# Attention's side work cut into pieces of three matmuls, spread over all 128 steps of an octet, and the last octet run block by block through both of its groups

## The chip, the cores and the metric

The kernel runs on one core of one Trainium2 chip. The metric is the device time of one execution in microseconds; the time before is 2678.99 us, the median of 3 runs (2677.80 to 2679.76). Engines are named as in the profile: PE is TensorE (PEld its weight loads), ACT is ScalarE, DVE is VectorE, POOL is GpSimd, and SP is the engine whose queue issues nearly all DMAs.

## The reference

Four residual layers on x of 2048 tokens by 512 features (32 heads of 16): softmax attention (A), hedgehog linear attention (B), A, B. Each layer is x + layer(layernorm(x)).

```python
# A
qkv = (x @ wqkv).reshape(B, S, 3, H, Dh).transpose(2, 0, 3, 1, 4)
p = softmax(einsum("bhqd,bhkd->bhqk", q, k) * Dh ** -0.5)
o = einsum("bhqk,bhkd->bhqd", p, v).transpose(0, 2, 1, 3).reshape(B, S, D) @ wo
# B
phi(t) = concat[softmax(t @ w_phi), softmax(-(t @ w_phi))]        # per head
kv = einsum("bhsf,bhsd->bhfd", phi(k), v);  z = sum over s of phi(k)
o = (phi(q) @ kv) / (phi(q) @ z + 1e-6) @ wo
```

The change touches layer A alone, which runs twice.

## The kernel before, in words

**Steps.** Layer A works on four *octets* of 8 heads. An octet has two *groups* of 4 heads, g = 2o (even heads) and g = 2o+1 (odd heads). A group goes through 4 blocks of 512 queries (`j`), and each block through 16 tiles of 128 keys (`kt`). One (g, j, kt) is a *step*; an octet has 128 steps, a layer 512. In a step, `scores` issues four matmuls `s<-kq` in two halves (two heads each, in the two row halves of the array), and ACT takes one exponential of 128x1024 for each half (`p<-s`). The halves go round three PSUM buffers (`psS`, `bufs=3`), the exponentials' results round six SBUF buffers. `pvs` then issues the four matmuls `pv<-p,v` of the step two back (`LAG = 2`); the trace records each as two. The 16 steps of a block add up in one PSUM bank, `pv`. After the last of them `norm` turns it around on DVE (`yt`, `rec`, `yn`), and for an odd group writes the octet's part of the attention's output (`yb`, `osp`) to DRAM, or for the last octet into `ob`. The bank is single: the next block's first `pv` matmul waits until DVE has read it (`yt`).

**Side work.** PE's order inside the attention is written out by hand (`tc.manual_schedule(engines={E.PE})`), while DVE, POOL and SP are ordered by a scheduler. Between the steps PE does other work in pieces. It comes from generators in the queue `self.fill`; `pump(1)` runs the first one up to its next `yield`. There are three kinds:

- `octet(o+1)`, during octet o: the values of the next octet's 8 heads (4 blocks of 48 matmuls of 128x128, `pv_`), then its keys and queries (8 projections of 12 matmuls of 128x512, `pqk`). A projection is read by DVE (`tq`, then the high half and the low half in `stg`), POOL squares the high half (`sq`), and one small matmul sums the squares per head (`psn`), which DVE reads (`km` or `sh`). `pqk`, `psn`, `pv_`, `po` and `pst` share one PSUM bank (tag "M").
- `tail(j, ob)`, in the last octet: the output projection of block j (4 tiles of 12 matmuls of 128x512, `po`), the residual (`xt`), the next layer's norm on DVE, and four transposes per tile (`pst`).
- `extra`, in the first layer alone: layer B's weights are folded and split (`prep_ao`, `prep_b`): 8 times four transposes (`bps`) and four fp32 matmuls (`bpf`) on PE, and a long run of work on DVE.

**Where the pieces stand before.** `values` yields after every 8 matmuls and once after its evacuation: 7 pumps a block, 28 in all. `project` yields after every 2, then there are three pumps without projection work, the third of which does `psn`: 9 a projection, 72 in all. An octet has thus 100 pumps, one in each of its steps 0 to 99; steps 100 to 127 have none. The tails yield every 4 matmuls. The last octet runs all of group 6 (steps 0 to 63) and then group 7 (64 to 127); a tail needs both groups of its block, so the first one starts at step 82, and block 3's is done after the attention, inside layer B's start (`nxt.feed`). `extra` starts in step 114 of the octet before.

**Loads of keys and queries.** `alloc_pairs` takes two SBUF tiles for a group's keys and queries (`kq`), `load_rows` copies rows of `stg` into them (12 DMAs) and `load_shift` four rows of `sh`. For the next octet's even group both were emitted in step 112, for its odd group at the start of that octet.

Of the kernel before, what the change touches and what calls it, by code (L numbers as in the profile page):

```python
# [33 lines left out]
LAG = 2  # L34
E = mybir.EngineType
COMPUTE = {E.PE, E.DVE, E.Activation, E.Pool}
# (part of the stationary side, part of the moving side): 0 = high, 1 = low half
# [4 lines left out]
def mha_hedgehog_stack(ctx, tc, x_in, a_wqkv, a_wo, b_wqkv, b_wphi, b_wo, out, shmin=SHMIN):  # L42
# [29 lines left out]
    # ones on the 16 rows of each head of an octet, column per head  # L72
# [7 lines left out]
    def peak_of(v, u, engine=None):  # L80
        """Bound on |v| per partition: the maximum, on the scalar engine the sum; v [P, 2048], its half u or all."""
        if u is not None:
            v = v[:, u * 1024:(u + 1) * 1024]
        m = sp.tile([P, 1], F32, name="pk")
        if engine is nc.scalar:
            junk = pp.tile([P, 1024], F32, tag="p", name="pkj")
            nc.scalar.activation(junk, v, AF.Abs, accum_out=m)
        else:
            nc.vector.tensor_reduce(m, v, AX.X, ALU.max, apply_absolute_value=True)
# [22 lines left out]
    def split(dst, src, sc):  # L112
        """dst[0] + dst[1] = src * sc, both fp16."""
# [30 lines left out]
    # rows 48..63 of each head's half: SHROW on the key side, 0 on the query side  # L144
# [14 lines left out]
    def prep_a():  # L159
        """The first layer up to its attention; splits wqkv on the side."""  # L160
# [12 lines left out]
        def octet(o):  # L173
            """High parts, and the scaled weights for the low parts."""
# [112 lines left out]
    # head order of B's columns: (octet, parity, four)  # L287
# [56 lines left out]
    class Norm:  # L344
# [8 lines left out]
        def stats_parts(self, t0, n, soon=False):  # L353
            """Mean and 1/deviation of tiles t0 .. t0+n-1."""
# [51 lines left out]
        def turned(self, t, n, ps):  # L406
            """Tiles t .. t+n-1, ps [P, n, 512]."""
# [27 lines left out]
        def half(self, t2):  # L435
            """As soon as two more tiles are there."""
# [58 lines left out]
    def norm2(ps, dst):  # L495
        """Both parities of an octet at once, ps [P, 2, 512]."""
# [13 lines left out]
    def o_block(j, ob, wo, co, x_src, x_dst, box, after=None, wide=True, early=False):  # L510
        """box receives the 4 new token tiles, after is called for each two.
        early: the first two tiles begin with the octets that come first."""
        for t2 in range(2):
# [12 lines left out]
            for u in range(0 if early and t2 == 0 else 2):  # L526
                t = 2 * t2 + u
                n = 0
                for a, b in PASSES:
                    yield  # L530
                    if n == 0:
                        ps = ps2[:, u, :] if wide else psum1("po")
                    for c in range(NC4):
                        nc.tensor.matmul(ps, ob[:, c, a, t * P:(t + 1) * P], wo[:, b, c, :], start=(n == 0), stop=(n == 11))  # L534
                        n += 1
# [14 lines left out]
    def v_block(xnT, wv, j):  # L550
        """Values of 4 token tiles, [V_h | 1] per head."""
# [19 lines left out]
    okt = cp.tile([32, 8], F32, name="okt")  # L571

    class LayerA:
# [14 lines left out]
        def start_octet(self, o, w):  # L588
            # [V_h | 1] per token tile and head
# [7 lines left out]
                stg=stgp.tile([P, 4, S], F16, tag="stg", name="stg"),  # kl, kh, qh, ql  # L597
# [4 lines left out]
        def project(self, o, j, ps, ten):  # L602
            n = 0
            for a, b in PASSES:
                for c in range(NC4):
                    nc.tensor.matmul(ps, self.oct[o]["w"][:, a, ten, c, :], self.xnT[j][:, b, c, :], start=(n == 0), stop=(n == 11))  # L606
                    n += 1
                    if n % 2 == 0:
                        yield

        def values(self, o, j, ps):
            """Values of 512 tokens for the octet's heads."""
            q = self.oct[o]
            n = 0
            for t in range(4):
                for a, b in PASSES:
                    for c in range(NC4):
# [3 lines left out]
                        if n % 8 == 0:  # L621
                            yield
# [43 lines left out]
        def octet(self, o):  # L666
            """Queries and keys of 8 heads, one PSUM bank at a time."""
            self.start_octet(o, self.next_w or self.octet_w(o))
            self.next_w = None
# [5 lines left out]
            for j in range(NJ):  # L675
                for ten in (1, 0):
                    ps = psum1("pqk")
                    yield from self.project(o, j, ps, ten)
# [8 lines left out]
                    yield  # L687
# [32 lines left out]
        def feed(self, lns, work):  # L720
            """All that comes before the attention; work[j]: pieces of other work around block j."""
# [106 lines left out]
        def tail(self, j, ob):  # L828
            xts = []
            ln = Norm(xts, f"a{self.li}_{j}")  # L830
            yield from o_block(j, ob, self.wo, con["oA"], self.x_src, self.x_dst, xts, ln.half, wide=False)
# [12 lines left out]
        def attention(self, extra, nxt):  # L844
            """All heads; returns the next layer's normalised input blocks as they are emitted."""
            state["att"] = True
            self.fill, self.pt, self.out = deque(), {}, []
            pend = deque()
            with tc.manual_schedule(engines={E.PE}):
                for g in range(8):  # L850
                    for k in range(NJ * NT):
                        j, kt = k // NT, k % NT
                        self.scores(g, j, kt)
                        pend.append((g, j, kt))
                        if len(pend) > LAG:
                            self.pvs(*pend.popleft())
                        if g % 2 == 0 and g < 6:
                            if k == 0:
                                if g:
                                    self.alloc_pairs(g + 1)  # L860
                                    self.load_pairs(g + 1)
                                self.fill.append(self.octet(g // 2 + 1))
                            self.pump(1)
                        elif g < 6:
                            if k < 48:
                                self.pump(1)
                            if k == 48:
                                while self.fill:
                                    self.pump(1)
                                self.alloc_pairs(g + 1)  # L870
                                self.load_pairs(g + 1)
                        if g == 5 and k == 50 and extra is not None:
                            self.fill.append(extra())
                        if g == 6:
                            if k == 8:
                                self.alloc_pairs(7)
                                self.load_pairs(7)
                            if k == 48:
                                self.wo = load_hl(dAo, "woA")
                                nxt.begin()  # L880
                        if g > 5 or (g == 5 and k > 50):
                            self.pump(1)
# [15 lines left out]
    class LayerB:  # L898
# [15 lines left out]
        def feed(self, j, xnT, between=lambda t: None):  # L914
            """Features and values of 512 tokens, summed into the state."""
# [66 lines left out]
        def expo(self, ps):  # L982
            """exp(x - max) and exp(min - x) per head."""
# [11 lines left out]
        def part_sums(self, f, r, factor):  # L995
            """factor / sum for the softmaxes r of a tile."""
# [7 lines left out]
        def share(self, f, factor):  # L1004
            """Both softmaxes of each head, times factor."""
# [3 lines left out]
        def halves(self, f):  # L1009
            """f = fk[0] + fk[1] in fp16."""  # L1010
# [6 lines left out]
        def share_split(self, f, low):  # L1017
            """share and halves for the last keys, in two parts side by side; low goes between."""
# [250 lines left out]
```

## Time and profile before

| | |
|---|---|
| median of 3 runs | 2678.99 us |
| span of the profiled execution | 2678.6 us |
| PE busy | 2555.4 us (95%) |
| ACT busy | 2214.8 us (83%) |
| DVE busy | 995.5 us (37%) |
| first layer A, its attention | 85.3 to 1101.7 us |
| second layer A, its attention | 1415.6 to 2419.4 us |

A matmul's end is modelled in this trace, and matmuls overlap: the useful number for PE is the distance from one start to the next, not the duration. A row of the timeline gives the start, the time it covers, engine, line, operation, output and inputs, shape and count. A row of the windows gives the stretch, its length, then busy time and count per engine, the granted share of the TensorE clock, the DMA share and GB/s. Time that an engine spends idle is named with what ended it, in brackets behind a row.

### The profile page before, as it was taken

To read this page: it belongs to the slowest core of one execution; us is meant where nothing else is said; L and a number is where in the kernel's file an instruction comes from. 1 tells how busy PE (TensorE), PEld (TensorE's weight loads), DVE (VectorE), ACT (ScalarE), POOL (GpSimd) and SP (SyncE) were. 2 spreads that over 40 slices of the span, in tenths; PEclk is the share of its full clock that TensorE was granted. 3 is DMA by queue.
4 is the path that set the end of the run, shared out by engine and by line. 5 is a ranking of instruction groups with operands and counts; after the bars stand their busy time and mean duration, and the time that the engine had idled before them with its cause. 6 is when DMAs were issued, how large, how long until landed. Compare 5 with 4: busy or idle time off the path is not lost.

```text
span 2678.6 us, 44388 instructions
## 1 busy us (share of the span) xinstructions
PE 2555.4 (95%) x18080; PEld 761.5 (28%) x18080; DVE 995.5 (37%) x1896; ACT 2214.8 (83%) x2442; POOL 373.6 (14%) x502
## 2 busy tenths in 40 slices
PE   6999999999999999999889999999999999999998
PEld 4321131122113122355343112211221111224543
DVE  6212112311224315689861122112112200248997
ACT  5799999999998997554438999999999999874552
POOL 3000000000000000266430000000000000004552
PEclk9999999999999999999999999999999999999999
DMA  4500310130122403100143004002200320121003
GB/s 150 102 29 13 51 30 9 17 56 9 48 32 73 127 27 99 40 24 9 65 103 67 4 14 64 9 9 40 41 5 29 62 50 1 36 72 48 9 17 104
DMA packets 48551, 120.05 MB, mean 45 GB/s; under 512 B 9872, under 2 KB 10768, under 8 KB 45136
## 3 DMA queue, kind: packets, MB, share of 16 engines
q1 hardware_dynamic: 47664, 114.75, 18.4%
q8 instruction: 144, 2.36, 0.4%
q0 software_dynamic: 672, 2.36, 0.2%
q14 instruction: 71, 0.58, 0.1%
HBM read 60.06 MB, written 31.59 MB: 34 GB/s over the span
## 4 chain that ended last, share of the span: by engine, by line
PE 61%; ACT 16%; DVE 14%; issue 6%; POOL 2%; DMA 0%; ACTq 0%; POOLq 0%; DVEq 0%
PE pv L811 26%; PE s L796 16%; ACT p L799 15%; PE pqk L606 6%; PE po L534 5%; DVE su L998 2%; PE pbv L927 1%; PE pk L927 1%; POOL f L1007 1%; DVE f L990 1%; DVE f L991 1%; DVE st L359 1%; DVE mx L987 1%; PE pq L927 1%; DVE su L999 1%
## 5 line engine op out<-in xcount | busy, mean ns | idle before, releaser
L799 ACT ACTIVATE p<-s 128x1024 f32<-128x1024 f32 x2048 | 1922.4, 1197 | 101.3 <-PE s L796 61.3
L811 PE MATMUL pv<-p,v 128*32 128x512 f32 x8192 | 1091.3, 605 | 2.9 <-DVE yt L473 2.8
L796 PE MATMUL s<-kq 64*128 64x512 f16 x4096 | 686.7, 383 | 39.6 <-DMA kq<-sh 3.3
L796 PEld LDWEIGHTS <-kq 64*128 64x128 f16 x4096 | 153.8, 94 | 720.7 <-issue 701.3
L473 DVE STREAM_TRANSPOSE yt<-pv 128x512 f32<-128x512 f32 x64 | 45.9, 716 | 768.8 <-PE pv L811 768.5
L811 PEld LDWEIGHTS pv<-p,v 128*32 128x32 f32 x8192 | 161.6, 108 | 360.6 <-issue 334.0
L633 POOL TENSOR_TENSOR sq<-stg 128x512 bf16<-128x512 f16 x48 | 71.1, 1481 | 1133.9 <-DVE stg L683 1052.0
L1007 POOL TENSOR_TENSOR f<-f,su 128x1024 f32<-128x1024 f32 x62 | 119.9, 1934 | 594.5 <-DVE su L1001 566.5
L682 DVE TENSOR_SCALAR tq<-pqk,c_qk 128x512 f32<-128x512 f32 x48 | 35.5, 740 | 324.1 <-PE pqk L606 324.1
L927 PEld LDWEIGHTS <-xnTa 128*128 128x128 f16 x1152 | 110.4, 98 | 137.8 <-DVE f L991 15.8
L606 PEld LDWEIGHTS <-wA 128*128 128x128 f16 x768 | 52.2, 99 | 277.0 <-issue 257.8
L606 PE MATMUL pqk<-xnTb,wA 128*128 128x512 f16 x384 | 110.2, 388 | 1.1 <-ACT xnTb L426 1.1
L606 PE MATMUL pqk<-xnT,wA 128*128 128x512 f16 x360 | 104.2, 383 | 3.9 <-DVE xnT L429 2.0
L927 PE MATMUL pbv<-wbv,xnTa 128*128 128x512 f16 x384 | 88.6, 379 | 12.1 <-DVE f L991 12.1
L534 PE MATMUL po<-woA,ob 128*128 128x512 f16 x384 | 97.0, 381 | 0.7 <-DVE ob L490 0.7
L992 ACT ACTIVATE f<-f,c_pB 128x1024 f32<-128x1024 f32 x64 | 72.6, 1148 | 29.7 <-DVE f L991 29.6
L1013 ACT ACTIVATE fk<-f 128x1024 f16<-128x1024 f32 x30 | 31.7, 1057 | 74.8 <-POOL f L1007 74.8
L927 PE MATMUL pk<-wbqk,xnTa 128*128 128x512 f16 x384 | 88.4, 379 | 0.0
L927 PE MATMUL pq<-wbqk,xnTa 128*128 128x512 f16 x384 | 88.4, 379 | 0.0
L998 DVE TENSOR_REDUCE su<-f 128x64 f32<-128x1024 f32 x64 | 77.5, 1211 | 9.5 <-ACT f L992 8.8
L1039 ACT ACTIVATE qT<-pqt 128x512 f32<-128x512 f32 x64 | 34.6, 592 | 54.1 <-PE pqt L1038 54.1
L534 PE MATMUL po<-wbo,obB 128*128 128x512 f16 x336 | 75.6, 385 | 3.3 <-DVE xnTb L429 3.3
(261 smaller groups left out, 1892.4 us busy)
## 6 DMA issues: line engine op xcount, KB each, us to landing
kq<-stg SPq DMA_DIRECT2D x168, 128.0 KB, 5.0
xd<-xt SPq DMA_DIRECT2D x24, 512.0 KB, 3.0
xt<-xd SPq DMA_DIRECT2D x24, 512.0 KB, 3.6
kq<-dC SPq DMA_DIRECT2D x64, 128.0 KB, 3.6
oD<-osp SPq DMA_DIRECT2D x24, 256.0 KB, 2.0
ob<-oD SPq DMA_DIRECT2D x8, 768.0 KB, 5.4
xt<-in_A_x_dram SPq DMA_DIRECT2D x8, 512.0 KB, 3.7
wbqk<-dBqk SPq DMA_DIRECT2D x2, 2048.0 KB, 8.9
```

What stands on the lines that cost most here:

```text
L473: nc.vector.transpose(yt.rearrange("p a b -> p (a b)"), ps)
L534: nc.tensor.matmul(ps, ob[:, c, a, t * P:(t + 1) * P], wo[:, b, c, :], start=(n == 0), stop=(n == 11))
L606: nc.tensor.matmul(ps, self.oct[o]["w"][:, a, ten, c, :], self.xnT[j][:, b, c, :], start=(n == 0), stop=(n == 11))
L633: nc.gpsimd.tensor_tensor(sq, hi, hi, ALU.mult)
L682: nc.vector.tensor_scalar(tq, ps, cqk, CLAMP, op0=ALU.mult, op1=ALU.min)
L796: nc.tensor.matmul(s[:, u, :], t[r:r + 64, 0, kt * P:(kt + 1) * P], t[r:r + 64, 1, j * 512:(j + 1) * 512], start=True, stop=True)
L799: nc.scalar.activation(pt, s, AF.Exp, scale=0.25 / (QS * QS))
L811: nc.tensor.matmul(acc[32 * hh:32 * hh + 32, :], self.oct[o]["v"][:, r:r + 32], pt[:, hh % 2, :], start=(kt == 0), stop=(kt == NT - 1), sk ...
L927: nc.tensor.matmul(dst, xnT[:, a, c, t * P:(t + 1) * P], w(b, c), start=(i == 0 and c == 0), stop=(i == 2 and c == NC4 - 1))
L992: nc.scalar.activation(f, f, AF.Exp, scale=con["pB"])
L998: nc.vector.tensor_reduce(su, f[:, r, :], AX.X, ALU.add)
L1007: nc.gpsimd.tensor_tensor(f3, f3, self.part_sums(f3, slice(0, 64), factor), ALU.mult)
```

## The change

1. `project` takes a `piece`; in the attention it is 3 instead of 2, and the last piece no longer ends in a pump of its own, so the evacuation by DVE follows the last matmul in the same pump. One of the two empty pumps between the evacuation and `psn` goes. A projection has 5 pumps instead of 9.
2. `values` yields after every 12 matmuls instead of 8: 4 pumps a block instead of 7. An octet has 56 pumps.
3. A counter, `credit`, grows by 56/116 each step, and a pump runs when it reaches 1: one in about 2.07 steps, up to step 118 (`FILLED`), where what is left is done at once.
4. In the last octet the order of the steps is block by block: block 0 of group 6, block 0 of group 7, block 1 of group 6 and so on. The first tail starts at about step 34. The tails of blocks 0 to 2 use pieces of 3 matmuls, block 3's of 4 as before; a pump comes in 0.65 of the steps.
5. Each octet's weights are loaded one octet ahead (`next_w`). The first 1536 columns of the next even group's rows are loaded once blocks 0 to 2 are projected, the rest and the shifts are emitted at step 118. Group 7 is loaded there too, and `extra` starts there.

The diff's core (comments and docstrings went as well, which moves the line numbers by 2 to 7):

```diff
-        def project(self, o, j, ps, ten):
+        def project(self, o, j, ps, ten, piece=2):
...
-                    if n % 2 == 0:
+                    if n % piece == 0 and n < 12:
                         yield
...
-                        if n % 8 == 0:
+                        if n % 12 == 0 and n < 48:
                             yield
...
-            self.start_octet(o, self.next_w or self.octet_w(o))
-            self.next_w = None
+            self.start_octet(o, self.next_w)
+            self.next_w = self.octet_w(o + 1) if o < 3 else None
...
                     sq = self.square(hi)
                     yield
-                    yield
                     self.norms(o, j, sq, ten)
+                    if j == 2 and ten == 0:
+                        self.alloc_pairs(2 * o)
+                        self.load_rows(2 * o, slice(0, 1536))
                     yield
...
+            credit = 0.0
+            order = [(g, j, kt) for g in range(6) for j in range(NJ) for kt in range(NT)]
+            order += [(g, j, kt) for j in range(NJ) for g in (6, 7) for kt in range(NT)]
...
+                    if o < 3:
+                        if k == 0:
+                            if o:
                                 self.alloc_pairs(g + 1)
                                 self.load_pairs(g + 1)
+                            self.fill.append(self.octet(o + 1))
+                        if k == FILLED:
+                            while self.fill:
+                                self.pump(1)
+                            self.load_rows(2 * o + 2, slice(1536, S))
+                            self.load_shift(2 * o + 2, slice(0, S))
...
+                        credit += 56 / (FILLED - 2)
+                    else:
...
+                        credit += 0.65
+                    if credit >= 1:
+                        credit -= 1
+                        self.pump(1)
```

What stands on PE in octet 1 of the first layer, where a projection's piece lies between two steps; `kq3` is the odd group's tile. Before, one step has the piece between its `pv` and the next step's scores:

```order
L811 MATMUL pv_4566<-p_4541,v1_1008 32x512 x2
L606 LDWEIGHTS wA_3299
L606 MATMUL pqk_4530<-xnT0_2_139,wA_3299 128x512
L606 LDWEIGHTS wA_3299
L606 MATMUL pqk_4530<-xnT0_2_139,wA_3299 128x512
L796 LDWEIGHTS kq3_0_3277
```

After, a piece has three matmuls, the step behind it has none, and the next piece follows a step later:

```order
L816 MATMUL pv_4559<-p_4657,v1_1033 32x512 x2
L609 LDWEIGHTS wA_1039
L609 MATMUL pqk_4694<-xnT0_2_139,wA_1039 128x512
L609 LDWEIGHTS wA_1039
L609 MATMUL pqk_4694<-xnT0_2_139,wA_1039 128x512
L609 LDWEIGHTS wA_1039
L609 MATMUL pqk_4694<-xnT0_2_139,wA_1039 128x512
L801 LDWEIGHTS kq3_0_3293
```

Pieces have one matmul more and stand in every second step.

DVE in the last octet of the first layer, from the split of the folded weights (`bhl`) to the first look at the value weights (`bwv`); `yt` is a block's end, on which PE's next block waits. Before:

```order
L118 SCALAR_TENSOR_TENSOR bhl1_8177<-bf1_7947,sB_sc_8140,bhl1_8177 128x2048
L473 STREAM_TRANSPOSE yt_8441<-pv_8061 128x512
L475 TENSOR_SCALAR rec_8443<-yt_8441 128x16
L476 RECIPROCAL rec_8443<-rec_8443 128x16
L480 TENSOR_TENSOR yn_8446<-yt_8441,rec_8443 128x16x16
L473 STREAM_TRANSPOSE yt_8673<-pv_8458 128x512
L475 TENSOR_SCALAR rec_8675<-yt_8673 128x16
L476 RECIPROCAL rec_8675<-rec_8675 128x16
L480 TENSOR_TENSOR yn_8678<-yt_8673,rec_8675 128x16x16
L89 TENSOR_REDUCE pk_8219<-bwv_8217 128x1
```

After:

```order
L120 SCALAR_TENSOR_TENSOR bhl0_8451<-bf0_7918,sB_sc_8418,bhl0_8451 128x2048
L120 SCALAR_TENSOR_TENSOR bhl1_8483<-bf1_8172,sB_sc_8418,bhl1_8483 128x2048
L91 TENSOR_REDUCE pk_8503<-bwv_8501 128x1
L103 TENSOR_SCALAR sBv_mm_8505<-sBv_mm_8505 128x1
L105 TENSOR_SCALAR sBv_es_8508<-sBv_mm_8505 128x1
L107 TENSOR_SCALAR sBv_sc_8510<-sBv_es_8508 128x1
L285 TENSOR_SCALAR c_oB_8624<-sBv_es_8508 128x1
L108 TENSOR_SCALAR sBv_sc_8510<-sBv_sc_8510 128x1
L117 TENSOR_SCALAR bhlv_8513<-bwv_8501,sBv_sc_8510 128x64 x2
```

Before, two blocks' ends stood between the two weight jobs; after, the jobs follow each other, and the next block's end stands behind both, and behind the first look at `bwo`.

More of the change, by code (lines that the diff above doesn't have):

```diff
@@ L34 @@
 LAG = 2
+STEPS = 2 * NJ * NT
+FILLED = 118
 E = mybir.EngineType
@@ L830, in tail @@
             ln = Norm(xts, f"a{self.li}_{j}")
-            yield from o_block(j, ob, self.wo, con["oA"], self.x_src, self.x_dst, xts, ln.half, wide=False)
+            yield from o_block(j, ob, self.wo, con["oA"], self.x_src, self.x_dst, xts, ln.half, wide=False, piece=3 if j < 3 else 4)
             yield from ln.steps()
@@ L877, in attention @@
                                 self.load_pairs(7)
[L878 to L882, printed above, removed]
+                                if extra is not None:
+                                    self.fill.append(extra())
+                        credit += 56 / (FILLED - 2)
+                    else:
+                        if k == 12:
+                            self.wo = load_hl(dAo, "woA")
+                        if k == 64:
+                            nxt.begin()
+                        credit += 0.65
```

42 lines of the change are left out of this document (13 added, 29 removed).

## The prediction

> **What bounds the kernel now.** The cores view gives the time to explain, the windows view the stages. The bounds are those of the octets, each 256 exponentials (`x` in the rows, a neighbour at the edge counted too).
>
> ```profile
> core 0: 2678.6 us, clock 0.994
> ```
>
> ```profile
> 85.30:333.00 247.70, 239.77 (x257) 0.99 0.21 39
> 333.00:580.30 247.30, 240.31 (x257) 1.00 0.15 24
> 580.30:836.30 256.00, 242.34 (x258) 1.00 0.17 36
> 836.30:1101.70 265.40, 239.82 (x256) 1.00 0.27 81
> 1415.60:2156.40 740.80, 720.12 (x769) 1.00 0.18 31
> 2156.40:2419.40 263.00, 239.96 (x257) 1.00 0.14 42
> ```
>
> The attention takes 2020 of 2679 us. Five octets are plain: the first, the second, and the three of the row of 740.80. Together they take 1235.8 us, 247.2 each. The third carries the start of layer B's weights, the fourth of each layer the tails. The second octet in four windows of 32 steps (length, then PE, PEld, DVE, ACT, POOL busy):
>
> ```profile
> 332.96:397.79 64.83, 64.83 (x586) 20.08 (x585) 7.74 (x15) 61.83 (x65) 0.00 (x0) 1.00 0.21 34
> 397.79:459.71 61.92, 61.92 (x434) 12.28 (x436) 13.61 (x24) 60.04 (x64) 5.92 (x4) 1.00 0.03 6
> ...
> 522.13:580.30 58.17, 54.63 (x387) 11.27 (x386) 12.38 (x20) 58.00 (x64) 1.82 (x3) 1.00 0.33 47
> ```
>
> With side work PE has no gap and ACT waits (the third window, left out, is like the second). In the fourth, nearly without, ACT has no gap and PE idles: 58.17/32 = 1.818 us a step. So the octet changes its bound at step 100. PE's step, from its timeline:
>
> ```profile
> 416.31 0.61 PE L606 MATMUL pqk<-xnT,wA 128*128 128x512 f16 x2
> ...
> 418.38 0.60 PE L606 MATMUL pqk<-xnT,wA 128*128 128x512 f16 x2
> 418.92 0.61 PE L796 MATMUL s<-kq 64*128 64x512 f16 x4
> ...
> 420.45 0.61 PE L796 MATMUL s<-kq 64*128 64x512 f16 x4
> ...
> 423.52 0.38 PE L641 MATMUL psn<-sq,bones 128*32 128x512 bf16 x1
> 423.83 0.71 PE L796 MATMUL s<-kq 64*128 64x512 f16 x4
> ...
> 425.47 0.60 PE L606 MATMUL pqk<-xnT,wA 128*128 128x512 f16 x2
> ```
>
> A step with a piece of two lasts 2.07 us (416.31 to 418.38), of which the piece is 0.54 (418.38 to 418.92). A step without is 1.53 (418.92 to 420.45), less than ACT's 1.818: behind a run of side work PE gets ahead of ACT for a while. `psn` adds 0.31; by 423.83 the lead is used up and the step lasts 1.64. Longer runs of the same matmuls, from the chain of waits and from a step of the first layer's last octet:
>
> ```profile
> 1355.68 10.36 PE po L534 x48
> ...
> 1371.86 2.68 PE pv__13261 L618 x48
> ```
>
> ```profile
> 1095.75 1.04 PE L534 MATMUL po<-woA,ob 128*128 128x512 f16 x4
> 1096.72 0.61 PE L796 MATMUL s<-kq 64*128 64x512 f16 x4
> ```
>
> A 128x512 matmul costs 10.36/48 = 0.216 us, one of 128x128 2.68/48 = 0.056. The piece of four takes 0.97, so 0.97 - 4 x 0.216 = 0.106 us go to each change to side work and back; the piece of two agrees (0.432 + 0.106 = 0.54).
>
> **The change part by part. Plain octets.** Before: 24 pieces of 8 values at 8 x 0.056 + 0.106 = 0.55, 48 pieces of two at 0.54, eight `psn` at 0.31: 41.5 us of side work. With 100 steps at 1.53 (153.4) and 28 ACT steps at 1.818 (50.9) that is 245.8; the octet takes 247.2, so 1.4 us are waits. After: 16 pieces of 12 values at 0.78, 32 of three at 0.754, eight `psn`: 39.0 us. They lie in 116 steps: 177.9 + 39.0 = 216.9, then 12 steps at 1.818 (21.8): 238.7. ACT needs 116 x 1.818 = 210.9 for the same steps, so PE stays the bound on average: two steps with one piece cost PE 3.82, ACT 3.64. Of the 7.1 us less, 4.5 come from 16 steps moved from ACT's rate to PE's, the rest from fewer changes.
>
> The waits after are not in the trace. At least 1.4 stay. Each `psn` ends a stretch of three light steps, where 0.1 is lost (1.64 against 1.53), eight times, and a double gap now and then adds as much; a block's end not followed by a piece leaves PE at `yt`. I take 3.3, nearer to the low end since the light steps above ran at 1.53; the high end, 6, is 1.4 and 0.6 for each `psn`. So 242.0, 5.2 less (2.5 to 7.1), five times: 26 us (12 to 36).
>
> **The wait for the squares.** One empty pump less stands between a projection's end and `psn`:
>
> ```profile
> 419.02 0.75 DVE L682 TENSOR_SCALAR tq<-pqk,c_qk 128x512 f32<-128x512 f32 x1 [11.86 <-PE pqk L606]
> ...
> 420.38 1.48 POOL L633 TENSOR_TENSOR sq<-stg 128x512 bf16<-128x512 f16 x1 [15.88 <-DVE stg L683]
> ```
>
> The square is done at 421.86. Two light steps behind the piece, PE stands at 418.92 + 2 x 1.535 = 421.99. It fits by 0.13 us, so I cost it at nothing; without that cover each delay of DVE is PE's, since `psn` stands ahead of the next step's scores in PE's order and ACT waits for those. Before, a delay had 1.5 us more to hide in.
>
> **Loads.** An even group's 12 row loads become 24, the last 12 of a quarter of the columns, behind the last projection (step 112 or 113). Layer A's start has such a set:
>
> ```profile
> 84.17 0.66 SPq L781 DMA_DIRECT2D kq<-stg  x1
> ...
> 91.28 0.59 SPq L783 DMA_DIRECT2D kq<-stg  x1
> 91.99 2.46 SPq L788 DMA_DIRECT2D kq<-sh  x4
> ```
>
> Twelve rows issue in 7.8 us, the shifts in 2.5 more; 13 steps at 1.818 give 23.6. SP's queue holds an `osp` store among them, done by about step 115. Hidden: nothing. The Trainium skill (DMA: Bandwidth & Descriptors, Rules for kernel authors) speaks against it: small transfers should be merged, under 64 KB one pays mostly overhead, and these carry 16 x 2 x 512 x 2 bytes = 32 KB. By that rule, 12 more an octet, exposed, would cost 6 x 7.8 = 47 us and leave 11 of the gain; the row agrees on the cost of each, but not that anyone waits for it.
>
> **Third octet.** It sheds most of `extra` and keeps two pieces of it: 242.0 + 2 = 244 against 256.0, 12 less (9 to 14 by the same ends).
>
> **Last octets.** The second layer's by 32 steps, and the weights' pieces in the first layer's:
>
> ```profile
> 2156.40:2215.00 58.60, 54.91 (x386) 11.56 (x385) 5.24 (x11) 58.60 (x66) 0.39 (x2) 1.00 0.25 57
> ...
> 2273.70:2342.20 68.50, 65.73 (x442) 14.92 (x441) 17.37 (x52) 60.86 (x66) 0.00 (x0) 1.00 0.10 32
> 2342.20:2419.40 77.20, 75.48 (x502) 18.53 (x500) 35.30 (x93) 61.79 (x64) 0.00 (x0) 1.00 0.21 72
> ```
>
> ```profile
> 837.31 1.16 PE L311 MATMUL bpf<-phi,bwt 128*128 128x128 f32 x8
> 838.40 0.60 PE L796 MATMUL s<-kq 64*128 64x512 f16 x4
> ...
> 839.93 0.66 PE L306 MATMUL bps<-ident,bw 128*128 128x128 f32 x4
> 840.52 0.61 PE L796 MATMUL s<-kq 64*128 64x512 f16 x4
> ```
>
> Half of it is at ACT's rate, then PE is overfull. After, each window but the first holds one tail: 32 x 1.534 + 16 x 0.754 + 4 transposes at 0.59 (840.52 - 839.93) = 63.5; the first stays at 58.6. With 1.5 for waits: 250.7 against 263.0, 12.3 less (9 to 14). In the first layer the first window also takes 14 weight pieces in 20 steps: 30.7 + 7 x 1.09 + 7 x 0.59 = 42.4, and 12 x 1.818: 64.2. There DVE matters:
>
> ```profile
> 848.88 2.29 DVE L89 TENSOR_REDUCE pk<-bf 128x1 f32<-128x2048 f32 x1
> ...
> 855.07 4.61 DVE L118 SCALAR_TENSOR_TENSOR bhl<-bf,sB_sc,bhl 128x2048 f16<-128x2048 f32 x2
> ...
> 902.10 2.28 DVE L89 TENSOR_REDUCE pk<-bwv 128x1 f32<-128x2048 f32 x1
> ...
> 917.10 2.27 DVE L89 TENSOR_REDUCE pk<-bwo 128x1 f32<-128x2048 f32 x1
> ```
>
> From 848.88 to 859.68 and from 902.10 to 919.37 DVE works 10.8 + 17.3 us, with 0.8 for the copies ahead 29. Before, blocks' ends lay between; after, all of it follows the last weight piece (step 19 of the octet) and stands ahead of `yt` of the block that ends at step 33, 25.2 us later. `yt` comes 4 us late, PE's next `pv` and the first tail wait, and with the splits of `bwo` ahead of `ob` I take 6 (0 to 12). So 64.2 + 190.6 + 1.5 + 6 = 262.3 against 265.4: 3.1 less (-3 to 9).
>
> **Ends.** After the attention DVE is on the chain:
>
> ```profile
> 1101.84 0.75 DVE L537 SCALAR_TENSOR_TENSOR xt<-po,c_oA,xt 128x512 f32<-128x512 f32 x1 [5.81 <-PE po L534]
> ...
> 1103.92 0.71 DVE L473 STREAM_TRANSPOSE yt<-pv 128x512 f32<-128x512 f32 x1
> ...
> 1109.74 1.00 DVE L401 TENSOR_SCALAR xn<-xt,mv,ly 128x512 f32<-128x512 f32 x2
> ```
>
> Block 2's norm stands there, 2.1 us ahead of `yt` and 1.0 of `xn`. After, its `po` is done three to five steps earlier; one or two transposes stay. 2.5 less at each of two ends (0 to 3).
>
> Sum: 26 + 12 + 12.3 + 3.1 + 5 = 58.4 us off 2678.6: 2620.2. The span is 0.4 under the median, so 2620 stands for the median too.
>
> **The rivals.** (1) Slower: light steps can't be short. With three score buffers, PE may not lead ACT, and a light step lasts 1.818 wherever it stands. An octet is then 48 x 2.29 + 8 x 1.85 + 72 x 1.818 = 255.6, 8.4 more; five make +42, the third octet +2, the last ones -4 and +9, the ends -5: 44 more, 2722. Against it: 420.45 shows 1.53 behind heavy steps. For it: 1.64 two steps later, and now every second step is light. It decides the sign where a light step costs 0.14 us more than 1.53, since there are about 430. 7%.
>
> (2) The squares come late: where DVE stands behind a block's end, `psn` waits 1 to 2 us. At 58.4/48 = 1.2 us each the gain is gone; 1.5 each gives 2692. DVE's order has `tq` next to a block's `yt` in about two of eight. 3%.
>
> (3) The weights jam DVE and waits are at their high ends: 12 + 9 + 9 - 3 + 0 = 27, 2650 or more. 7%.
>
> (4) The clock. The Trainium skill (TensorE: Matmul & The Clock Gate, A second HAM failure mode: psum-queue depth-cycling) says that frequent short idles of PE between groups of matmuls can make the clock swing to half. Here the window 522.13 to 580.30 has 3.5 us of such idles at a granted 1.00, so the trace doesn't bear it out. As a mechanism here: a light step at half speed is 3.07, 1.5 more; a tenth of the 430 would cost 65 us, 2685. 1%.
>
> (5) Better than 2602: waits as before, no jam: 36 + 14 + 14 + 9 + 5 = 78. 3%. (6) The loads come late after all: half or all of the 7.8 us exposed, six times, is 23 to 47: 2643 to 2667. 2%.
>
> **How the numbers follow.** The forecast has 77%, at 2620; its bounds taken together would be 2600 to 2650, and the ends rarely meet, so from 2602, and up to 2652, which takes in the nearer part of (3) and (6): of the rivals' 23% some 19 stay outside. 0.2% (5.4 us) is about what a measurement can tell from no change. Faster: 77 + 7 + 3 + 2 = 89%. Within 0.2%: 3%, of (1) and (2). Slower: 8%, the rest of (1), (2) and (4).
>
> **What would show it.** In the profile after, a plain octet takes about 242 us, its windows of 32 steps some 62, 61, 61 and 59; side work reaches step 115; `psn` starts without a wait for `sq`. The last octet's windows are 59, 64, 64, 64, with a wait of `pv` for `yt` of some us near step 34 in the first layer. The prediction is wrong if a light step behind a piece of three takes 1.8, if PE waits at `psn` in most projections, or at an octet's first scores for `kq`.

## The result, and the profile after

The changed kernel takes 2628.78 us, the median of four runs (2628.22 to 2631.21), against 2678.39 us for the kernel before, the median of four (2675.71 to 2679.76): a ratio of 0.9816, with a 95% interval of 0.9802 to 0.9830. The forecast was 2620 us, with a range of 2602 to 2652. The profiled execution has a span of 2626.4 us, 52.2 less than before; the forecast was 58.4.

The cores view, and then the windows of the kernel after by octet, cut at the exponentials' starts as the prediction cut those of before (length, ACT busy and its number, granted clock, DMA share, GB/s):

```profile
core 0: 2626.4 us, clock 0.991
```

```profile
83.70:326.30 242.60, 238.66 (x256) 0.99 0.22 40
326.30:568.60 242.30, 238.96 (x257) 1.00 0.16 25
568.60:811.90 243.30, 239.49 (x258) 1.00 0.23 41
811.90:1079.70 267.80, 241.67 (x257) 0.98 0.23 81
1390.10:2117.40 727.30, 716.41 (x769) 1.00 0.19 33
2117.40:2370.80 253.40, 240.53 (x257) 1.00 0.13 45
```

Against the rows of before, the five plain octets lose 23.6 us (1235.8 to 1212.2), the third octet 12.7, the second layer's last 9.6. The first layer's last octet, though, became 2.4 us longer, and it is the only one whose granted clock is below 0.99. The stretches between the first attention and the second (313.9 before, 310.4 after) and behind the second (259.2, 255.6) lose 3.5 and 3.6, and 1.6 go ahead of the first attention, where nothing was changed (in the runs below that start varies from 84.0 to 85.8, against 83.7 here and 85.3 before). Together: 23.6 + 12.7 + 9.6 - 2.4 + 7.1 + 1.6 = 52.2.

The second octet in windows of 32 steps (PE, PEld, DVE, ACT, POOL busy) shows the new shape; the second and third of the four are alike:

```profile
326.30:388.50 62.20, 61.59 (x578) 19.77 (x576) 7.38 (x15) 60.72 (x65) 0.00 (x0) 1.00 0.21 31
388.50:448.80 60.30, 59.99 (x429) 12.56 (x431) 11.14 (x21) 59.52 (x64) 4.44 (x3) 1.00 0.05 11
...
509.10:568.60 59.50, 57.43 (x413) 11.98 (x415) 14.75 (x26) 59.12 (x65) 3.30 (x4) 1.00 0.25 40
```

The forecast was 62, 61, 61 and 59. PE and ACT are now both busy nearly all the time: in the second window PE lacks 0.3 us of 60.3 and ACT 0.8, where before PE lacked nothing and ACT 1.9 of 61.9. The mechanism is seen step by step in PE's timeline of that octet:

```profile
410.65 0.60 PE L801 MATMUL s<-kq 64*128 64x512 f16 x4
...
412.18 0.60 PE L801 MATMUL s<-kq 64*128 64x512 f16 x4
...
413.71 0.82 PE L609 MATMUL pqk<-xnT,wA 128*128 128x512 f16 x3
414.47 0.60 PE L801 MATMUL s<-kq 64*128 64x512 f16 x4
...
416.00 0.61 PE L801 MATMUL s<-kq 64*128 64x512 f16 x4
```

The light steps take 1.53 us (410.65 to 412.18, 414.47 to 416.00), the one with a piece of three 2.29 (412.18 to 414.47), of which the piece is 0.76. The first rival, in which a light step lasts ACT's 1.818 and an octet 255.6, is refuted: the octet takes 242.3.

### The profile page after: what moved, and what is told of

It is laid out like the page before. It is cut to its first block, busy times and chain, and to the rows that moved or that the text cites. A ratio compares the mean times of both kernels' runs of the same rounds, so it can differ in the third digit from the quotient of the medians.

```text
span 2626.4 us, 44484 instructions
## 1 busy us (share of the span) xinstructions
PE 2509.6 (96%) x18080; PEld 756.7 (29%) x18080; DVE 1005.7 (38%) x1902; ACT 2204.9 (84%) x2436; POOL 374.6 (14%) x502
## 4 chain that ended last, share of the span: by engine, by line
PE 74%; DVE 14%; ACT 6%; issue 3%; POOL 2%; DMA 1%; ACTq 0%; POOLq 0%; SPq 0%; DVEq 0%
PE pv L816 34%; PE s L801 19%; PE pqk L609 6%; PE po L537 5%; ACT p L804 5%; DVE su L1005 1%; PE pk L934 1%; PE pbv L934 1%; PE pq L934 1%; DVE yt L475 1%; POOL f L1014 1%; DVE st L361 1%; DVE f L997 1%; PE pn L1074 1%; DVE su L1006 1%
## 5 line engine op out<-in xcount | busy, mean ns | idle before, releaser
L801 PE MATMUL s<-kq 64*128 64x512 f16 x4096 | 652.2, 382 | 19.1 <-DMA kq<-sh 3.1
L801 PEld LDWEIGHTS <-kq 64*128 64x128 f16 x4096 | 143.8, 93 | 705.6 <-issue 689.2
L609 PEld LDWEIGHTS <-wA 128*128 128x128 f16 x768 | 59.5, 98 | 217.1 <-issue 173.8
L540 DVE SCALAR_TENSOR_TENSOR xt<-po,c_oA,xt 128x512 f32<-128x512 f32 x32 | 23.3, 730 | 211.6 <-PE po L537 211.6
L609 PE MATMUL pqk<-xnTb,wA 128*128 128x512 f16 x384 | 101.8, 387 | 1.1 <-ACT xnTb L428 1.1
L609 PE MATMUL pqk<-xnT,wA 128*128 128x512 f16 x360 | 95.8, 382 | 3.1 <-DVE xnT L431 2.6
```

The source lines that it names most:

```text
L801: nc.tensor.matmul(s[:, u, :], t[r:r + 64, 0, kt * P:(kt + 1) * P], t[r:r + 64, 1, j * 512:(j + 1) * 512], start=True, stop=True)
```

## The experiments

Each is an edit of the kernel after. Lengths of octets are read as above, from one profile of each run. The kernel before, timed again beside the runs, took 2677.5 to 2680.0 us (medians), so differences of 2 to 3 us between two runs' times say little.

**All side work at the octet's start.** It asks whether the gain comes from the even spreading or from the fewer changes to side work.

```diff
-                        credit += 56 / (FILLED - 2)
+                        credit += 1
-                    if j == 2 and ten == 0:
-                        self.alloc_pairs(2 * o)
-                        self.load_rows(2 * o, slice(0, 1536))
-                            self.load_rows(2 * o + 2, slice(1536, S))
+                            self.alloc_pairs(2 * o + 2)
+                            self.load_rows(2 * o + 2, slice(0, S))
```

> The wide pieces stay, but one is given to every step from the octet's first on, until none is left; the rows are loaded whole at step 118. Theory (the spreading carries the gain, since it moves steps from ACT's rate to PE's): an octet is 56 x 1.534 + 39.0 + 72 x 1.818 = 255.8 us, with 1.5 for waits 257, against 242.5; six octets give 87 more, 2715. Rival (the fewer changes to side work carry it): an octet is the one of before less 2.6, 244.7, and the kernel 2642.

Measured: 2776.16 us (2774.06 to 2776.65), 1.0359 of before (1.0342 to 1.0376). It is worse than the theory said: 268.2 us an octet, not 257. The windows of the second octet:

```profile
353.00:430.00 77.00, 72.81 (x620) 22.57 (x619) 15.38 (x27) 62.80 (x66) 4.43 (x3) 1.00 0.14 22
430.00:504.40 74.40, 66.70 (x452) 13.87 (x451) 19.57 (x32) 60.94 (x64) 7.40 (x5) 1.00 0.11 14
504.40:562.50 58.10, 54.45 (x383) 11.40 (x383) 4.97 (x11) 58.10 (x65) 0.00 (x0) 1.00 0.29 39
```

The waits view of that octet (total, times, longest) has the rest:

```profile
PE psn L644 <- POOL sq L636: 11.1, 8, 1.4
```

The second half runs at ACT's 1.815 us a step, as reckoned. In the first, every `psn` waits 1.4 us for its squares, since a pump at every step leaves one step ahead of it and not two: 255.8 + 11.1 = 266.9, and 1.3 for other waits. So the spreading carries the gain, and it also hides the squares. The rival at 2642 falls.

**The old pieces, spread.**

```diff
-                    if n % piece == 0 and n < 12:
+                    if n % 2 == 0:
-                            if n % 12 == 0 and n < 48:
+                            if n % 8 == 0:
                     sq = self.square(hi)
                     yield
+                    yield
-                        credit += 56 / (FILLED - 2)
+                        credit += 100 / (FILLED - 2)
```

> The spreading stays, but the pieces are those of before (8 values, two matmuls, two empty pumps ahead of psn). Theory: only the changes to side work come back, 24 x 0.55 + 48 x 0.54 against 16 x 0.78 + 32 x 0.754 = 2.5 us an octet, 15 for six: 2644. Rival (a piece of every second step needs the width, since PE is the bound only on average): the octets go back to 247.3 and the kernel to 2658 or above.

Measured: 2643.07 us (2641.49 to 2645.07), ratio 0.9863 (0.9846 to 0.9879). The plain octets take 244.6 us on average, 2.2 more than with wide pieces. The two causes of the plain octets' gain are thus parted: some 2.2 of the 4.7 us are fewer changes to side work, the rest is the spreading. For 24 changes less that is 0.09 us each, near the 0.106 that came out of rows of the kernel before.

**The weights' pieces sooner.** This and the fifth run ask why the first layer's last octet did not gain.

```diff
-                        credit += 0.65
+                        credit += 1 if extra is not None and k < 20 else 0.65
```

> In the first layer's last octet the weights' pieces go one to each of the first 20 steps, not one to 0.65. Theory (DVE's weight work, late by some 4 us at the block that ends at step 33, makes the 11 us step and the half clock behind it): DVE is done ahead of that block, the step falls from 11.0 to 2.7 us and the next ten steps lose another 1 to 2 us of half clock: 7 to 10 less, 2619 to 2622. Rival (PE's own side work fills this octet): the pieces cost the same wherever they stand, and the kernel stays at 2626 to 2631, the wait moving to another block.

Measured: 2627.64 us (2627.21 to 2629.21), ratio 0.9809 (0.9792 to 0.9825): no gain. The rival's words hold, that the wait moves to another block. DVE's and PE's timelines show it at the block that ends at step 17:

```profile
851.65 4.61 DVE L120 SCALAR_TENSOR_TENSOR bhl<-bf,sB_sc,bhl 128x2048 f16<-128x2048 f32 x2
856.18 2.28 DVE L91 TENSOR_REDUCE pk<-bwv 128x1 f32<-128x2048 f32 x1
858.38 0.70 DVE L475 STREAM_TRANSPOSE yt<-pv 128x512 f32<-128x512 f32 x1
```

```profile
859.13 1.94 PE L816 MATMUL pv<-p,v 128*32 128x512 f32 x8 [5.26 <-DVE sBv_mm L103]
```

`yt` stands behind the weights' split and maximum, and the next block's `pv` behind `yt`. So my theory was half right: DVE's weight work makes the stall, but starting it sooner here only chose another block end. What has to change is its length in one piece.

**The rows in one go.** The early part of three quarters of the rows is taken away, the pieces stay.

```diff
-                    if j == 2 and ten == 0:
-                        self.alloc_pairs(2 * o)
-                        self.load_rows(2 * o, slice(0, 1536))
-                            self.load_rows(2 * o + 2, slice(1536, S))
+                            self.alloc_pairs(2 * o + 2)
+                            self.load_rows(2 * o + 2, slice(0, S))
```

> No early part of three quarters of the rows: all 12 rows of an even group are loaded whole behind step 118. Theory (SP's issues are hidden either way: 7.8 us for the rows and 2.5 for the shifts before the next octet 18 us later): no change, within 3 us, 2626 to 2632. Rival (the split is needed): the last rows land after the octet's end, 2 to 8 us late in six octets, 2640 to 2677. Rival (12 small transfers fewer pay): 5 us less or more.

Measured: 2629.45 us (2628.65 to 2630.18), ratio 0.9814 (0.9798 to 0.9830): no change. Neither the 12 further loads nor their small size cost anything here, and with ten steps left the split into two parts gains nothing.

**The weights' work woven in.** The scale and split of the values' and the output's weights need nothing of PE; they are given out between the 16 pieces that do.

```diff
+        def beside():
+            esv, scv = scale_of([flat(wv)], "sBv")
+            yield
...
+                    if c % 2:
+                        yield
...
                 nc.vector.tensor_copy(wt, pst)
+                next(side, None)
                 yield
```

> The weights' work on DVE that needs nothing of PE (the scale and the split of the values' and of the output's weights) is given out in pieces of some 2 us between the 16 pieces on PE, not all behind them; pieces on PE as in the kernel after. Theory (one block end in the first layer's last octet finds DVE behind up to 29 us of weight work; starting earlier only moved it to the block that ends at step 17): DVE's longest run falls to some 12 us, the 11 us step and the half clock go, 7 to 10 less: 2619 to 2622, that octet 258 to 260. Rival (the weights' transfers or PE's own pieces fill this octet): it stays at 267 and the kernel at 2626 to 2631.

Measured: 2620.75 us (2620.17 to 2622.02), ratio 0.9789 (0.9774 to 0.9804): 8 us below the kernel after, as expected. Its second window of that octet, and DVE at the block that ended in the stall:

```profile
878.70:944.00 65.30, 63.52 (x448) 13.70 (x445) 21.19 (x57) 60.64 (x65) 0.00 (x0) 1.00 0.14 47
```

```profile
881.52 0.72 DVE L486 STREAM_TRANSPOSE yt<-pv 128x512 f32<-128x512 f32 x1 [13.40 <-PE pv L827]
```

DVE now waits 13.4 us for PE, not PE for DVE; the window falls from 74.6 to 65.3 us, and the clock stays at 1.00. The cause is shown.

**A gap in the tails.**

```diff
             for t in range(4):
                 yield
+                if t == 1:
+                    yield
...
-                        credit += 0.65
+                        credit += 0.7
```

> In the last octets one empty pump stands between a tail's first and second transpose, and pumps come at 0.7 a step, not 0.65. Theory (the second transpose waits 1.2 us for DVE, where the evacuation of the first stands behind the norm's small operations): two to three tails a layer, 1.2 us each, 5 to 7 less in all: 2622 to 2624, the second layer's last octet 250 to 251. Rival (the wait moves to the next transpose, or ACT is the bound there): within 2 us of the kernel after, 2627 to 2631.

Measured: 2618.64 us (2617.43 to 2620.90), ratio 0.9780 (0.9766 to 0.9793): 10 less, more than the theory gave. The second layer's last octet goes from 253.4 to 251.4, 1.9 less and not 2 to 3. Of the 6.4 us of the first layer's (267.8 to 261.3) some 5 are the stall, shorter here: `pv` waits 2.57 us and `po` 1.64, and the clock stays at 1.00. In the second layer's first tail the transposes are now 3.65 us apart (the first at 2224.94), DVE has emptied the bank at 2228.21, and PE's row of the second shows no wait:

```profile
2224.94 0.66 PE L418 MATMUL pst<-ident,xn 128*128 128x128 f32 x4
...
2227.52 0.69 DVE L431 TENSOR_TENSOR xnTa<-pst,xnTa 128x512 f16<-128x512 f32 x1
...
2228.59 0.66 PE L418 MATMUL pst<-ident,xn 128*128 128x128 f32 x4
```

The edit changes the gap and the rate at once, and a mere shift of the pumps does nearly as much: with the tails untouched that octet takes 251.4 in the run with the old pieces spread, 251.8 in the dense one and 251.6 in the one after this, and one such wait of 1.2 us is left in each, where the kernel after has two. How much the empty pump gives by itself is not shown.

**Room ahead of the squares.**

```diff
                     sq = self.square(hi)
                     yield
+                    yield
-                        credit += 56 / (FILLED - 2)
+                        credit += 64 / (FILLED - 2)
```

> The second empty pump ahead of psn comes back (64 pumps an octet, over the same 116 steps). Theory (the squares are done just as PE comes to psn, so their wait costs nothing but three late cases of together 4 us): 0 to 4 less, 2625 to 2629. Rival (the squares hold PE up at every psn, hidden in the profile's modelled ends): 0.3 us or more at 48 of them, 2614 or less.

Measured: 2630.10 us (2628.92 to 2631.21), ratio 0.9823 (0.9809 to 0.9836): no gain, and 1 us above what the theory gave. The plain octets are 0.4 to 2 us longer, the first layer's last octet 7.4 shorter: its stall is down to one wait of 2.56 us ahead of `pv`, with the pieces shifted once more. The three late cases in the kernel after are 0.50, 0.81 and 0.49 us, 1.8 together and not 4; one of 0.81 is left here. So the squares cost next to nothing: the rival at 2614 falls.

**More steps of side work.** The edit is one number, 122 and in a later run 126.

```diff
-FILLED = 118
+FILLED = 122
```

> The side work is spread over 120 steps of an octet, not 116. Theory (each step moved from ACT's rate to PE's gives 1.818 - 1.534 = 0.28 us, and the loads are still hidden: 7.8 us of rows and 2.5 of shifts in 6 steps of 1.82): 4 x 0.28 x 6 = 6.8 less, 2622. Rival (the last rows, issued by 10.3 us and landing 2 to 5 later, come after the octet's end at 10.9): 2 to 5 us late in six octets, 2634 to 2652.

Measured: 2628.90 us (2625.62 to 2631.26), ratio 0.9813 (0.9800 to 0.9827). The second octet of each layer goes from 242.3 to 241.1, 1.2 less as the theory has it. But the weights' pieces, which wait for step 122, now begin later, and the first layer's last octet gets 2.1 longer (one `pv` waits 9.26 us there). The third octet gets 2.8 longer for another reason: one `psn` waits 2.46 us for its squares, at 756.12, and the granted clock is 0.50 for 3.4 us behind it; the same `psn` waits 0.81 in the kernel after, without a dip. Together that takes back what the plain octets gave, and neither the theory's 2622 nor the rival's number came.

> The side work is spread over 124 steps, so that the last projection ends two steps ahead of the octet's end. With 122 the last row load is issued 8 us ahead of the next octet's first scores; four steps of 1.82 later that leaves less than the 2 us that such a load takes to land. Theory (loads cost nothing as long as they land in time, and no more than their delay then): 1.1 gained and 1 to 3 lost in each of six octets against 122: 2626 to 2640. Rival (loads still hidden): 2622 or less. Rival (all of an octet's 10.3 us of issues exposed): 2670 or more.

Measured: 2636.19 us (2633.49 to 2637.05), ratio 0.9836 (0.9821 to 0.9852), inside what the theory gave. The waits view has PE's waits for the shifts (`sh`), which are loaded behind the rows (total, times, longest):

```profile
PE s L801 <- DMA kq<-sh: 7.4, 9, 3.3
```

Of these 3.3 us are the attention's very first wait, 2.8 in the kernel after. The other eight, 4.1 us, are new and stand at three octets' starts, 2.2 of them at the second octet's. That octet takes 244.0 us, 2.9 more than with 122, so the loads cost little beyond their delay. The first layer's last octet is long too, 271.3, as one `pv` waits 12.57 us for `yt` there.

**The last octet in the old order.**

```diff
-            order = [(g, j, kt) for g in range(6) for j in range(NJ) for kt in range(NT)]
-            order += [(g, j, kt) for j in range(NJ) for g in (6, 7) for kt in range(NT)]
+            order = [(g, j, kt) for g in range(8) for j in range(NJ) for kt in range(NT)]
...
-                        credit += 0.65
+                        credit += 1
```

The tails' pieces are of four matmuls again.

> The last octet goes as before, group by group, with pieces of four and a pump at every step; the other octets as after. Theory (block by block through both groups puts three tails into steps at PE's rate and takes block 2's norm off the chain): the second layer's last octet goes from 253.4 back to 263 and each of the two ends loses its 3.5 us: 8 to 10, 7 and as much as -3 to 0 in the first layer's last octet, where the weights stand early in the octet as in the third run: 2640 to 2646. Rival (the smaller pieces and the rate carry it, not the order): 2627 to 2632.

Measured: 2655.28 us (2652.59 to 2656.37), ratio 0.9906 (0.9891 to 0.9921). The second layer's last octet is back at 262.6 (+9.3), and its last two windows are within 0.1 us of those of before (68.5 and 77.2):

```profile
2249.60:2318.10 68.50, 65.74 (x442) 14.93 (x441) 17.34 (x52) 60.87 (x65) 0.00 (x0) 1.00 0.10 31
2318.10:2395.40 77.30, 75.59 (x504) 18.54 (x502) 35.27 (x93) 61.83 (x64) 0.00 (x0) 1.00 0.21 73
```

The two ends lose 3.2 and 3.4. So far the theory holds; the 9 us above its range are the first layer's last octet, 276.8 us. The stall sits at step 17 there, with pumps at every step, as in the third run (267.2 us), and this edit costs 9.6 us on top, as in the second layer, which the theory had left out. With these 9.0, and 3.0 in the first octets and the start, the 27.9 us of span are complete. The edit takes back the order, the size of the pieces and the rate together, so it doesn't show what the order is worth alone: the rival is not put to the test.

**All that helped.** Woven weights, the gap in the tails, and 122 or 124 for `FILLED`, but 118 in the octet in which the weights begin.

```diff
+                        filled = 118 if o == 2 and extra is not None else FILLED
...
-                        if k == FILLED:
+                        if k == filled:
...
-                        credit += 56 / (FILLED - 2)
+                        credit += 56 / (filled - 2)
```

> The woven weights, the empty pump in the tails at 0.7 a step, and 120 steps of side work, but 116 in the octet in which the weights begin. The parts add up if each takes another wait: 8 for the weights, 1.9 for each of two last octets, 1.1 for each of five octets: 17 to 18 less than after, 2611. Rival (they share a wait, since the first layer's last octet gained from a shift of its pieces in two runs already): 2616 to 2619.

> As the run before, with 122 steps of side work. Theory (0.28 us a step, the loads still in time): 0.57 for each of five octets, 3 less than the run before, 2608. Rival (the loads are late in some octets): as the run before or up to 5 more.

Measured: 2616.84 us (2615.98 to 2618.10), ratio 0.9767 (0.9754 to 0.9780), and 2617.03 us (2614.90 to 2618.63), ratio 0.9766 (0.9752 to 0.9779). Both are faster than the two kernels compared here. For both the rival's number holds. The second octet takes 241.1 and 240.9 us: two more steps gave 0.1 there, not 0.57, and no loads are late. In the first run the shortfall is not a shared wait alone: the first layer's last octet gives 8.2 us of the 9.9 hoped for, the second's all of its 1.9, and the first layer's third octet takes 246.4 us, 3.1 more than in the kernel after. The timelines of POOL and PE show what stands there:

```profile
746.76 3.01 POOL L649 TENSOR_TENSOR sq<-stg 128x512 bf16<-128x512 f16 x1 [20.18 <-DVE stg L699]
...
749.82 0.54 PE L657 MATMUL psn<-sq,bones 128*32 128x512 bf16 x1 [2.46 <-POOL sq L649]
```

It is one `psn` whose squares come late, the second rival's wait. The square takes 3.01 us and not 1.48, beside a split of the output projection's weights on DVE (`ahlo`, 2.35 us from 746.53). It is as long in the kernel after, but there PE has three steps between the projection's last piece and `psn`, and waits 0.81; here, with 122 alone and with 124 it has two, and waits 2.46. So where the pumps fall decides it.

## Why the prediction was right, and where it was not

**Plain octets: right.** Forecast 242.0 each, measured 242.1 to 243.0; 23.6 us for five against 26. The third octet, forecast at 244, takes 243.3. The spread old pieces and the dense wide ones confirm both of its terms.

**The wait for the squares: cost nearly right, its cover thinner than said.** DVE, POOL and PE in the second octet:

```profile
403.45 0.75 DVE L685 TENSOR_SCALAR tq<-pqk,c_qk 128x512 f32<-128x512 f32 x1 [10.51 <-PE pqk L609]
...
404.81 1.48 POOL L636 TENSOR_TENSOR sq<-stg 128x512 bf16<-128x512 f16 x1 [79.91 <-DVE stg L686]
...
406.34 0.38 PE L644 MATMUL psn<-sq,bones 128*32 128x512 bf16 x1
```

The square ends at 406.29 and `psn` starts 0.05 us later, where I had 0.13. The row shows no wait; of the 48, three do, 1.8 us in all, and the run with a second empty pump gains nothing. The dense run, with a step less, pays 1.4 us at each.

**Loads: right.** In the kernel after only the first layer's very first scores wait for `kq`; later only weight loads of PE do, three times and by 0.84 us at most. The Trainium skill (DMA: Bandwidth & Descriptors, Rules for kernel authors) would merge such small transfers; whole rows in half as many loads gave 2629.45 against 2628.78, so the runs show nothing for that rule where no one waits.

**The second layer's last octet: the mechanism right, a size off by 2.7 us.** Forecast 250.7 with windows of 59, 64, 64, 64; measured:

```profile
2117.40:2175.60 58.20, 54.73 (x383) 11.45 (x383) 5.24 (x11) 58.20 (x65) 0.38 (x2) 1.00 0.13 43
2175.60:2241.40 65.80, 63.97 (x450) 13.95 (x453) 21.20 (x57) 61.15 (x66) 0.00 (x0) 1.00 0.14 45
2241.40:2305.80 64.40, 63.69 (x452) 13.95 (x448) 22.27 (x59) 60.58 (x65) 0.00 (x0) 1.00 0.14 46
2305.80:2370.80 65.00, 63.47 (x452) 13.94 (x446) 21.71 (x58) 60.60 (x65) 0.00 (x0) 1.00 0.13 45
```

The term that was too small is "1.5 for waits". A tail's first transpose, the one at 2231.49, meets the norm that its own last `po` began:

```profile
2228.53 0.75 DVE L540 SCALAR_TENSOR_TENSOR xt<-po,c_oA,xt 128x512 f32<-128x512 f32 x1 [10.52 <-PE po L537]
...
2231.49 0.66 PE L418 MATMUL pst<-ident,xn 128*128 128x128 f32 x4
...
2233.36 0.68 DVE L426 CAST xnTa<-pst 128x512 f16<-128x512 f32 x1
2234.07 0.69 DVE L431 TENSOR_TENSOR xnTa<-pst,xnTa 128x512 f16<-128x512 f32 x1
...
2234.91 0.63 PE L418 MATMUL pst<-ident,xn 128*128 128x128 f32 x4 [1.23 <-DVE xnTa L431]
```

The copy out of the bank waits on DVE behind that norm until 2233.36, and the next transpose 1.23 us for the bank. The first and the third of this octet's tails have this wait, 2.45 us together, and with the empty pump and the rate of 0.7 both are gone and the octet is 1.9 shorter. The ends gained 7.1 in all, 3.5 and 3.6, where I had 2.5 each and 3 at most; the run in the old order gives 6.6 of them back.

**The first layer's last octet: the step that failed.** I put a wait of 4 us of `yt`, "6 (0 to 12)" in all, and forecast 3.1 less; it came out 2.4 more. Place and cause were right. The octet's second window, which has the stall, and the rows of DVE, SP's queue and PE at the block that ends at step 33:

```profile
875.80:950.40 74.60, 65.82 (x448) 13.86 (x444) 31.15 (x90) 60.85 (x66) 0.65 (x3) 0.93 0.29 101
```

```profile
880.13 2.28 DVE L91 TENSOR_REDUCE pk<-bwo 128x1 f32<-128x2048 f32 x1
882.33 0.71 DVE L475 STREAM_TRANSPOSE yt<-pv 128x512 f32<-128x512 f32 x1
```

```profile
882.86 0.45 SPq L829 DMA_DIRECT2D ob<-oD  x1
```

```profile
883.10 1.94 PE L816 MATMUL pv<-p,v 128*32 128x512 f32 x8 [3.77 <-DVE sBo_mm L103]
888.26 1.46 PE L537 MATMUL po<-woA,ob 128*128 128x512 f16 x3 [3.23 <-DMA ob<-oD]
```

The 4 us are there (3.77). What follows was put too low: the tail's load of `ob`, and not the splits of `bwo`, ends the next wait, going out at 882.86 and landing some 5 us later, another 3.23; and the clock was not in the sum. The window view by single microseconds (PE busy, granted clock, DMA share, GB/s):

```profile
879.00:880.00 1.00, 0.32 (x2) 1.00 0.00 0
880.00:881.00 1.00, 0.00 (x0) 0.97 0.34 139
881.00:882.00 1.00, 0.00 (x0) 0.50 1.01 410
...
890.00:891.00 1.00, 1.00 (x8) 0.50 1.03 426
891.00:892.00 1.00, 1.00 (x10) 0.91 0.47 188
```

PE runs at half speed for 10 us: the eight `pv` take 1.94 us and not 1.06, the first `po` 1.46 and not 0.82. The same window of the second layer, without the weights, takes 65.8, so the stall cost 8.8 us where I had 6, inside the 0 to 12. That is 2.8 of the 5.5 us by which the octet missed its 262.3; the other 2.7 are again the term of 1.5 for waits, as in the second layer. The weaving removes 7.9 us of this octet and leaves 259.9.

**The rivals.** The first fell. The second came at three of 48 `psn` alone, 1.8 us in all. The third, the weights' jam, came in this one octet but not with the high ends elsewhere. The clock's dips came from long waits, not from many short ones: the plain octets, full of short ones, hold 0.99 to 1.00. The loads came late only with 126.

## What to carry to other kernels

Where two engines take turns as the bound, spread the side work so that both stay just busy, and cost it by the step: here 0.28 us for every step moved from one engine's rate to the other's, and some 0.1 for each change of matmul that is saved. Ask of work on a third engine not how much it is but how long its longest piece is, and who comes to its queue behind it; moving such a piece changes who waits and how long (2.6 to 12.6 us in the runs above), cutting it up ended the wait. A small shift of one schedule moved this stall by some microseconds to either side, so time an edit's parts by the stretch that they touch, not by the kernel's time alone.

## What the runs showed of the hardware that was not expected

The granted clock halved soon after PE stopped, and came back only after some microseconds of work. In the kernel after, the last matmul ahead of the stall ends at 879.33 and the clock is at 0.50 from about 881, some 1.6 us later; the burst of 1.94 us at 883.10 did not lift it, and it is back some 2.9 us after 888.26. In the run with the weights' pieces sooner, PE stops at 853.87:

```profile
855.00:856.00 1.00, 0.00 (x0) 1.00 0.93 393
856.00:857.00 1.00, 0.00 (x0) 0.58 0.99 393
...
862.00:863.00 1.00, 1.00 (x10) 0.50 1.02 393
863.00:864.00 1.00, 1.00 (x16) 1.00 1.27 463
```

There it takes 2.3 us down and, from 859.13, 3.9 us up. The Trainium skill (TensorE: Matmul & The Clock Gate, What's actually happening) gives a window of some 3.4 us that runs freely, one idle for the way down and one busy for the way up. The way up is near that; the way down began before a whole window without a matmul had passed in both cases, so here the measurement decides. A shorter wait can already cost the clock: in three runs (122 alone, and both of the last two) the wait of 2.46 us in the third octet was followed by 0.50 for 3.4 us. It need not: through the wait of 2.57 us ahead of `pv` in the run with the gap the clock stayed at 1.00. What decides between the two is not shown.
